# Attention and a mixture of experts on one core: how a pair of heads is turned back, projected and divided

## The chip, the cores and the metric

One core of one Trainium2 chip runs the whole program. The metric is the device time of one execution in microseconds (us); lower is better. TensorE (PE) multiplies and transposes into PSUM, VectorE (DVE) and ScalarE (ACT) read PSUM, GpSimd (POOL) works in SBUF alone, and SyncE (SP) issues most of the transfers.

## What is computed

Attention with rotary embedding over 8 batches, 8 heads, 576 positions and 64 dimensions, and then a top-1 mixture of 8 experts (512 to 1024 to 512) over the 4608 tokens. Cut to what matters:

```
q_rot, k_rot = rotate(q), rotate(k)
scores = q_rot @ k_rot.T / sqrt(64)
attn = exp(scores - max); attn = attn / (sum(attn) + 1e-9)
x = attn @ v                       # to 4608 x 512
logits = x @ w_gate; e = argmax(logits); gate = softmax(logits)[e]
eom = sigmoid(x @ w_output_gate)
out[token] = gate * eom[e] * (relu(x @ w1[e]) @ w2[e])
```

## The kernel before

The program is first attention, then experts. Attention goes through 32 pairs of heads, four to a batch (`NP` = 4). A pair has nine steps; a step computes the scores of 128 queries of one head against all 576 keys (`scores`, L464; one step serves the last 64 queries of both heads, L457), takes their maximum on DVE (`peak`, L470) and the exponential on ACT (`exp`, L479), and one step later DVE transposes the result in blocks of 32 (`turn`, L485). Operands are split into a rounded high part and a remainder, so that each product is three matmuls. Scores have two PSUM buffers; the exponential frees one.

`values` (L507) multiplies the turned exponentials by v. It gives the pair's output with the 2 x 64 dimensions on the partitions and the 576 queries along the free axis, in the one PSUM tile `acc` (4 banks). To store tokens by rows it must be turned back. `evict` (L514 to L516) copies `acc` to SBUF (`ac`) on ACT, as five chunks of queries: four of 128 and one of 64. `back` (L522) turns each chunk and computes its logits in one matmul of 160 moving columns: the chunk is the stationary operand, and the moving operand `ii` is the identity (128 columns) beside the weights of both gates for both heads (32 columns, `BW` = 160 in all). The operands are full fp32, and each such matmul runs as two instructions of TensorE with a load of weights each. `divide` multiplies the result, read from `acc`, by the reciprocal sums `rz` into the token tile `xb`: three instructions on DVE (L530: four chunks, L532: their logits, L535: logits of the fifth chunk) and two on ACT (L539: the fifth chunk, one for each head). Then the `values` of the next pair can use `acc`.

The order of the work is written out by hand. `EVENTS` gives each part a step and a phase. In one step come the scores, the maximum and the exponential, then what is listed in phase 1 (`back` among it), then the `turn` of the step before, then phase 2 (`divide` among it), then phase 3. Within a phase the parts come in the order in which they were listed. Each engine executes its instructions in this order.

Routing (`place`) runs once per batch, spread over the steps of the following pairs with a list of its own (`fs`). Two of its matmuls on TensorE borrow free columns of a later pair's `acc`: the ranks (`s14`, L655 and L656, read on DVE by `s14b`, L660 and L661, which also adds `base`, made on POOL by L643) and the token lists (`s20`, L695, read on DVE by `s21`, L698). Both fall into a step in which a pair is turned back, `s14` and `s20` in phase 1 just ahead of `back`, and their readers in phase 3. With pairs counted from 0, the ranks meet every fourth pair from the sixth (5, 9, ... 29), the lists every fourth from the eighth (7, 11, ... 31). `ones` (L685 on DVE, L687 on POOL) falls into the steps after pairs 6, 10, ... 30. `own` holds the tiles that two pairs use in turn.

Of the kernel before, what the change touches and what calls it, by code (L numbers as in the profile page):

```python
# [10 lines left out]
F32 = mybir.dt.float32  # L11
# [3 lines left out]
AF = mybir.ActivationFunctionType  # L15
ALU = mybir.AluOpType
# [3 lines left out]
S, H, D = 576, 8, 64  # L20
NP = H // 2
DM = H * D
E, FF = 8, 1024
P = 128
HS = S // 2
QM = 512
QR = S - QM
NCH = 5
XW = DM + 1

HL = 2 * E
RW = DM + H * HL

BW = P + 2 * HL
# [8 lines left out]
NB, TAIL, PE_, PO = S // 32, 160, 192, 0  # L43
# [74 lines left out]
def body(ctx, tc, nb, offs, qk, v, rope, cst, gates, w, out):  # L118
    nc = tc.nc
    NT = nb * S  # L120

    def pool(st, n, b, **k):
        return st.enter_context(tc.tile_pool(name=n, bufs=b, **k))


    early, main, scores = ExitStack(), ExitStack(), ExitStack()
    cpool = pool(ctx, "cpool", 1, side="left")
    dpool = pool(ctx, "dpool", 1, space=bass.MemoryType.DRAM)
    px, px2 = pool(ctx, "px", 1, side="left"), pool(ctx, "px2", 2, side="left")
    pa2 = pool(main, "pa", 2, side="left")  # L130
    pp1, pp2 = pool(early, "pp", 1, side="right"), pool(early, "pp2", 2, side="right")
    ps_a = pool(main, "ps_a", 1, space=PSUM, side="left")
    ps_s = pool(scores, "ps_s", 2, space=PSUM, side="right")

    small = Small(ps_s)
    pools = px, px2, pa2, pp1, pp2, ps_s, small, ps_a

    xd = dpool.tile([NT, XW], F32, name="xd")

    nl = E * list_rows(nb) // P  # L140
    lst = [dpool.tile([nl, P], F32, name=f"lst{c}") for c in range(2)]

    first = Pair.first(tc, pools, qk[0, 0], rope)
    ident = cpool.tile([P, P], F32, name="ident")
    make_identity(nc, ident)
    o = offs[C_TRI]
    ct = cpool.tile([P, o], F32, name="ct")
    cc = lambda i: ct[:, offs[i]:offs[i + 1]]

    stage = pa2.tile([P, 2, S], F32, tag="stage", name="stage", bufs=1).rearrange("p a b -> p (a b)")  # L150
    nst = offs[-1] - o
    sc = lambda i: stage[:, offs[i] - o:offs[i + 1] - o]

    ii = cpool.tile([P, NP, BW], F32, name="ii")
    trib = cpool.tile([P, P], BF16, name="trib")
    oneb = cpool.tile([P, P], BF16, name="oneb")
    cnt = cpool.tile([P, E], F32, name="cnt")

    row = cpool.tile([P, nl], BF16, name="row")
    lists = cpool.tile([P, nl], F32, name="lists")  # L160
    zero = stage[:, nst:nst + 256]
    nc.vector.memset(zero, 0.0)
    nc.scalar.dma_start(out=ct, in_=cst[:, 0:o])
    nc.scalar.dma_start(out=stage[:, 0:nst], in_=cst[:, o:])
    nc.scalar.dma_start(out=ii[:, :, P:].rearrange("p n (h x) -> p n h x", h=2), in_=gates)


    consts = [
        lambda: nc.vector.tensor_copy(ii[:, :, 0:P], ident.unsqueeze(1).broadcast_to((P, NP, P))),
        lambda: nc.vector.tensor_copy(trib, sc(C_TRI)),  # L170
        lambda: nc.vector.tensor_copy(oneb, sc(C_ONE)),
        lambda: nc.vector.tensor_copy(row, sc(C_ROW)),
        lambda: (nc.vector.memset(cnt, 0.0), nc.vector.memset(lists, 0.0)),
    ]

    att = Attention(tc, nb, pools, cc, ident, ii, first, trib, oneb, cnt, zero, qk, v, xd, row, lists)
    n0 = slot_counts(nb)[0]
    moe = Moe(tc, nb, (px, px2, small), cc, ident, cnt, w, xd, lists, lst, out)

    if n0:  # L180
        g = att.done(nb - 3) + 1
        for k, f in enumerate(pieces(moe.table0(), 18)):
            att.at(g + k, 2, f)
        att.at(g + 18, 2, moe.fetch)
    att.start(consts)
    for g in range(att.G):
        att.step(g)
    early.close()
    if n0:
        moe.open_right(pool(ctx, "mr", 1, side="right", reuse_waits="tile"))  # L190
        moe.begin0()
    for g in range(att.G, att.G + TURN):
        att.step(g)
    scores.close()
    small.move(pool(ctx, "ps_x", 2, space=PSUM, side="right", reuse_waits="tile"))
    moe.ph = pool(ctx, "ps_h", 1, space=PSUM, side="right", reuse_waits="tile")
    if not n0:
        att.rest(lambda g: True)
        main.close()
        moe.open_right(pool(ctx, "mr", 1, side="right", reuse_waits="tile"))  # L200
        left = []
    else:

        att.rest(lambda g: g <= att.G + 1)
        for u in range(3):
            moe.split(u)
        att.rest(lambda g: g <= att.G + 8)
        for h in range(2):
            moe.turn(0, h)
        for j in range(2):  # L210
            moe.products(0, j)
        att.rest(lambda g: True)
        main.close()
    moe.open_left(pool(ctx, "ml", 1, side="left", reuse_waits="tile"),
                  pool(ctx, "ps_m", 1, space=PSUM, side="left", reuse_waits="tile"))
    if n0:
        left = att.last + pieces(moe.table1(), 60)
    else:
        for f in att.last + pieces(moe.table1(), 60):
            f()  # L220
        moe.fetch()
        moe.begin0()
        moe.begin1()
    moe.run(left)
# [7 lines left out]
class Attention:  # L232


    def __init__(self, tc, nb, pools, cc, ident, ii, first, trib, oneb, cnt, zero, qk, v, xd, row, lists):
        nc = tc.nc
        px, px2, pa2, pp1, pp2, ps_s, small, ps_a = pools
        NT = nb * S
        own = []
        self.inits = []  # L240

        def init(bd, z, rz):
            nc.gpsimd.tensor_copy(bd.rearrange("p a b -> p (a b)"), zero)
            nc.gpsimd.memset(z, 1.0)
            nc.gpsimd.memset(rz, 1.0)

        for i in range(2):
            o = (px.tile([P, 2, P], F32R, name=f"bd{i}"), px.tile([P, 2 * NCH], F32, name=f"z{i}"),
                 px.tile([P, 2 * NCH], F32, name=f"rz{i}"), px.tile([P, 1], F32, name=f"no{i}"))
            self.inits.append(lambda o=o: init(*o[0:3]))  # L250
            own.append(o)
        npair = nb * NP
        self.G, self.pairs = 9 * npair, []
# [88 lines left out]
class Pair:  # L342


    def __init__(self, tc, pools, n, own, ident, ii, rt, qk, v):
        self.tc, self.nc = tc, tc.nc
        self.px, self.px2, self.pa, self.pp1, self.pp2, self.ps_s, _, self.ps_a = pools
        self.bd, self.z, self.rz, self.no = own
        self.n, self.nm, self.hp = n, f"{n}", n % NP
        self.ident, self.ii, self.rt, self.qkd, self.vd = ident, ii, rt, qk, v  # L350
        self.raw = None
# [157 lines left out]
                                 skip_group_check=True)  # L509

    def evict(self):
        ac = self.ac = self.pa.tile([P, NCH, 4, 32], F32, tag="ac", name=f"ac{self.nm}")
        main = self.acc[:, :, 32:TAIL].rearrange("p a (c x) -> p c a x", x=32)
        self.nc.scalar.copy(ac[:, 0:4, :, :], main)  # L514
        self.nc.scalar.copy(ac[0:D, 4, 0:2, :], self.acc[0:D, 0:2, TAIL:PE_])
        self.nc.scalar.copy(ac[D:P, 4, 0:2, :], self.acc[D:P, 2:4, 0:32])  # L516

    def back(self):

        for c in range(NCH):  # L520
            n, o = (P, PO) if c < 4 else (QR, PO + BW)
            self.nc.tensor.matmul(self.acc[0:n, c % 4, o:o + BW], self.ac[:, c, :, :].rearrange("p a x -> p (a x)")[:, 0:n],  # L522
                                  self.ii[:, self.hp, :], start=True, stop=True, skip_group_check=True)

    def divide(self, xb):
        nc, V, acc, rz = self.nc, self.nc.vector, self.acc, self.rz
# [8 lines left out]
        V.tensor_tensor(out=xb[0:QR, 4, l0:l0 + 2 * HL].rearrange("p (h x) -> p h x", x=HL),  # L535
                        in0=last[:, P:BW].rearrange("p (h x) -> p h x", x=HL),
                        in1=rz[0:QR, 8:10].unsqueeze(2).broadcast_to((QR, 2, HL)), op=ALU.mult)
        for h in range(2):
            nc.scalar.activation(xb[0:QR, 4, x0 + h * D:x0 + h * D + D], last[:, h * D:h * D + D], AF.Copy,  # L539
                                 scale=rz[0:QR, 8 + h:9 + h])  # L540


def number(NT, b):
# [5 lines left out]
def place(tc, pools, pairs, b, NT, cc, trib, oneb, cnt, xbs, xd, row, lists):  # L549

    nc = tc.nc
# [70 lines left out]
    def s10():  # L622
        V.tensor_scalar(T["eg"], T["eg"], 1.0, None, op0=ALU.add)

    def s11():
        tt(out=T["eg"], in0=T["eg"], in1=T["sm"], op=ALU.mult)

    def s12():
        nc.vector.reciprocal(T["eg"], T["eg"])
# [36 lines left out]
    def s16():  # L666
        nc.vector.tensor_reduce(new("po", [P, NCH]), T["pr"], axis=AX.X, op=ALU.add)
# [42 lines left out]
    def adds(*cs):  # L710
        return lambda: [add(c) for c in cs]

    fs = [(0, 2, s0), (2, 2, s1), (3, 2, s2), (5, 2, s3), (8, 2, s4), (9, 2, s5), (10, 2, s6), (11, 2, s7), (12, 2, add0),
          (12, 2, adds(1, 2)), (13, 2, adds(3, 4)), (15, 2, s8), (15, 2, base), (17, 1, s14), (17, 3, s14b), (18, 2, s9),
          (19, 2, lambda: (s10(), s11())), (20, 2, s15), (22, 2, lambda: (s16(), s12())), (23, 2, s17), (35, 1, s20), (35, 3, s21)]
    fs += [(26 + c, 3, lambda c=c: ones(c)) for c in range(NCH)]

    if b == NT // S - 2:
# [449 lines left out]
```

## Time and profile before

| | |
|---|---|
| time, median of 3 runs | 1104.14 us (1101.99 to 1106.68) |
| the profiled execution, its own time | 1111.51 us |
| its span, first to last instruction | 1109.7 us |
| PE busy | 1027.9 us (93%) |
| DVE busy | 827.9 us (75%) |
| ACT busy | 644.7 us (58%) |
| POOL busy | 604.1 us (54%) |
| mean granted clock of TensorE | 0.971 |

Busy time is the union of an engine's instructions. Matmuls are pipelined, so that the records of neighbours overlap; what one costs is read from start to start. Loads of weights are listed as PEld. The attention part runs to about 600 us, the experts behind it.

### The profile page before, as it was taken

What the parts mean: (1) busy time and instruction counts of PE and PEld (TensorE: products, weight loads), DVE (VectorE), ACT (ScalarE), POOL (GpSimd) and SP (SyncE); (2) the same over time, 40 slices, a digit from 0 to 9 for tenths busy, and PEclk for the clock granted to TensorE, in tenths of its full rate; (3) what the DMA queues carried; (4) which work ended last, traced back from release to release, by engine and by line L of the source; (5) the groups of instructions that cost most, each with busy time, mean ns of one, the idle gap of its engine ahead of it and who ended that gap; (6) DMA issues with size and microseconds to landing.
All of it is one profiled execution on the core that took longest, in us unless ns stands there. A gap on an engine that the chain in (4) does not pass through costs nothing.

```text
span 1109.7 us, 34896 instructions
## 1 busy us (share of the span) xinstructions
PE 1027.9 (93%) x14465; PEld 890.5 (80%) x14465; DVE 827.9 (75%) x1357; ACT 644.7 (58%) x1345; POOL 604.1 (54%) x592
## 2 busy tenths in 40 slices
PE   3999999999999999999976998899999999999995
PEld 3788877877877787787766987798899889889885
DVE  6788888888888688788764775656767867876782
ACT  3466666666666465566453553455757756766772
POOL 4667887887978688688531051112532632632621
PEclk9999999999999899899888998999999999999998
DMA  5545555555746455545266585556887888888870
GB/s 184 162 129 164 167 165 145 152 166 159 199 126 174 114 167 173 130 145 159 51 184 210 199 302 184 190 171 193 301 291 252 286 286 292 265 305 304 256 274 27
DMA packets 58562, 216.48 MB, mean 195 GB/s; under 512 B 9405, under 2 KB 10012, under 8 KB 54304
## 3 DMA queue, kind: packets, MB, share of 16 engines
q1 hardware_dynamic: 50304, 194.03, 55.9%
q0 software_dynamic: 6496, 18.92, 4.8%
q8 instruction: 115, 1.88, 0.7%
q10 hardware_dynamic: 1600, 1.26, 0.4%
q14 instruction: 47, 0.39, 0.1%
HBM read 196.04 MB, written 20.24 MB: 195 GB/s over the span
## 4 chain that ended last, share of the span: by engine, by line
PE 65%; DVE 12%; issue 10%; DMA 6%; ACT 4%; POOL 2%; SPq 1%; POOLq 0%; ACTq 0%; DVEq 0%
PE py L1045 15%; PE sc L464 15%; PE acc L507 14%; PE ph L1002 11%; PE ph L994 4%; DVE m L470 3%; DVE pt L485 3%; DMA out<-y,0idx 3%; ACT pm L479 2%; PE acc L522 2%; PE sc L457 2%; PE mtp L980 1%; DVE wl L966 1%; DMA v<-in_v 1%; DVE xb L530 1%
## 5 line engine op out<-in xcount | busy, mean ns | idle before, releaser
L479 ACT ACTIVATE pm<-sc,m 128x576 f32<-128x576 f32 x288 | 213.5, 741 | 192.9 <-DVE m L470 191.3
L966 DVE TENSOR_TENSOR wl<-wr,wh 128x1024 fp32r<-128x1024 f32 x183 | 254.6, 1403 | 48.1 <-ACT wh L964 46.5
L470 DVE TENSOR_REDUCE m<-sc 128x1 f32<-128x576 f32 x288 | 213.2, 740 | 85.8 <-PE sc L464 70.7
L464 PE MATMUL sc<-kh,q 64*128 64x288 f32 x1024 | 227.7, 330 | 26.4 <-ACT pm L479 11.7
L507 PE MATMUL acc<-pt,v 32*64 32x160 f32 (+1 forms) x9216 | 203.0, 303 | 19.2 <-DMA v<-in_v 5.2
L485 DVE STREAM_TRANSPOSE pt<-pm 128x576 f32<-128x576 f32 x288 | 220.0, 764 | 0.3 <-ACT pm L479 0.3
L1045 PE MATMUL py<-wh,ht 128*128 128x512 f32 x640 | 214.9, 400 | 0.0
L964 ACT CAST wh<-wr 128x1024 fp32r<-128x1024 f32 x208 | 212.7, 1050 | 0.4 <-DMA wr<-in_w 0.4
L464 PEld LDWEIGHTS sc<-kh,q 64*128 64x128 f32 x1024 | 154.1, 195 | 69.5 <-ACT pm L479 26.1
L507 PEld LDWEIGHTS acc<-pt,v 32*64 32x64 f32 x9216 | 163.2, 135 | 43.8 <-issue 21.3
L1002 PE MATMUL ph<-xt,wh 128*128 128x256 f32 x896 | 166.4, 289 | 7.3 <-DVE ht L1020 5.8
L413 POOL TENSOR_TENSOR raw<-raw,rt 128x1152 f32<-128x1152 f32 x62 | 164.1, 2647 | 8.3 <-DMA raw<-in_qk 8.0
L1002 PEld LDWEIGHTS ph<-xt,wh 128*128 128x128 f32 x896 | 143.7, 197 | 9.7 <-issue 6.1
L1045 PEld LDWEIGHTS py<-wh,ht 128*128 128x128 f32 x640 | 120.6, 188 | 24.8
L1002 PE MATMUL ph<-xt,wl 128*128 128x256 f32 x448 | 128.5, 287 | 0.0
L1045 PE MATMUL py<-wl,ht 128*128 128x512 f32 x320 | 125.7, 393 | 0.0
L966 POOL TENSOR_TENSOR wl<-wr,wh 128x1024 fp32r<-128x1024 f32 x25 | 61.3, 2450 | 110.6 <-ACT wh L964 108.2
L464 PE MATMUL sc<-kl,q 64*128 64x288 f32 x512 | 112.6, 302 | 0.6 <-issue 0.6
L417 POOL TENSOR_TENSOR raw<-raw 128x576 f32<-128x576 f32 x62 | 88.1, 1421 | 2.4
L1019 ACT ACTIVATE ht<-ph 128x512 fp32r<-128x512 f32 x56 | 33.5, 598 | 96.1 <-PE ph L1002 96.1
L1002 PEld LDWEIGHTS ph<-xt,wl 128*128 128x128 f32 x448 | 88.6, 198 | 0.0
L464 PEld LDWEIGHTS sc<-kl,q 64*128 64x128 f32 x512 | 86.0, 196 | 0.9 <-issue 0.9
(245 smaller groups left out, 1329.3 us busy)
## 6 DMA issues: line engine op xcount, KB each, us to landing
wr<-in_w SPq DMA_DIRECT2D x208, 512.0 KB, 5.5
raw<-in_qk SPq DMA_DIRECT2D x64, 576.0 KB, 4.7
v<-in_v SPq DMA_DIRECT2D x128, 288.0 KB, 5.2
xd<-xb SPq DMA_DIRECT2D x16, 513.0 KB, 4.9
xd<-xb SPq DMA_DIRECT2D x8, 128.2 KB, 4.3
rt<-in_rope ACTq DMA_DIRECT2D x1, 576.0 KB, 5.6
xg<-xd,2idx POOLq DMA_INDIRECT x18, 6.8
out<-y,2idx POOLq DMA_INDIRECT x18, 5.2
```

Of the source, the lines that this page charges most:

```text
L413: self.eng(eng).tensor_tensor(out=rv, in0=rv, in1=self.rt[:, 2 * t:2 * t + 2, x], op=ALU.mult)
L417: self.eng(eng).tensor_tensor(out=r[:, 2 * t, x], in0=r[:, 2 * t, x], in1=r[:, 2 * t + 1, x], op=ALU.add)
L464: nc.tensor.matmul(ps[:, a, :HS], self.q[r, w, c * P:c * P + P], mov[r, a * HS:a * HS + HS], start=(n == 0), stop=(n == 2))
L470: nc.vector.tensor_reduce(self.m[i], ps[:, :, :HS], axis=AX.XY, op=ALU.max, negate=True)
L479: nc.scalar.activation(pe.rearrange("p (a b) -> p a b", a=2), self.ps[i][:, :, :HS], AF.Exp, bias=self.m[i], scale=1.0, accum_out=self.z[: ...
L485: self.nc.vector.transpose(out=self.pt[:, st[0] + 5 * st[1] if st else 4, :], in_=self.pc.pop(i))
L507: nc.tensor.matmul(self.acc[h * D:h * D + D, a, o:o + 32 * n], self.v[r, h, j, :], self.pt[r, u:u + n, 32 * j:32 * j + 32], start=(j == 0) ...
L964: self.nc.scalar.copy(wh, r)
L966: eng.tensor_tensor(out=wl, in0=r, in1=wh.bitcast(F32), op=ALU.subtract)
L994: nc.tensor.matmul(ph[:, 0, :], st[:, dc, 0:P], mv[:, dc, :], start=(n == 0), stop=(n == 11))
L1002: nc.tensor.matmul(ph[:, f, :], st[:, dc, fs], mv[:, dc, :], start=(n == 0), stop=(n == 11))
L1045: self.nc.tensor.matmul(py[h], st[:, f, hs], mv, start=(f == 0 and n == 0), stop=(f == 7 and n == 2))
```

## The change

`back` becomes two loops: five transposing instructions of TensorE (the chunk against the 128-column identity `ident`), and then five matmuls that multiply the same chunks by the gate weights alone, with 32 moving columns. `ii` holds only those 32 columns for each of the four pairs of a batch, and the DVE copy of the identity into it (L169) is gone. The fifth chunk is handled with 128 columns like the others: `ac` becomes a tile of `own`, whose fifth chunk POOL fills with zeros once at the start. The two divisions on ACT become one on DVE. `s14b` and `s21` move from phase 3 to phase 2, where they are listed ahead of `divide`.

```diff
-    ii = cpool.tile([P, NP, BW], F32, name="ii")
+    ii = cpool.tile([P, NP, 2 * HL], F32, name="ii")
...
-    nc.scalar.dma_start(out=ii[:, :, P:].rearrange("p n (h x) -> p n h x", h=2), in_=gates)
+    nc.scalar.dma_start(out=ii.rearrange("p n (h x) -> p n h x", h=2), in_=gates)
...
-        lambda: nc.vector.tensor_copy(ii[:, :, 0:P], ident.unsqueeze(1).broadcast_to((P, NP, P))),
...
+        def init(bd, z, rz, ac):
+            nc.gpsimd.memset(ac[:, NCH - 1, :, :], 0.0)
...
-                 px.tile([P, 2 * NCH], F32, name=f"rz{i}"), px.tile([P, 1], F32, name=f"no{i}"))
+                 px.tile([P, 2 * NCH], F32, name=f"rz{i}"), px.tile([P, NCH, 4, 32], F32, name=f"ac{i}"))
...
-        ac = self.ac = self.pa.tile([P, NCH, 4, 32], F32, tag="ac", name=f"ac{self.nm}")
+        ac = self.ac
...
+        parts = []
         for c in range(NCH):
-            n, o = (P, PO) if c < 4 else (QR, PO + BW)
-            self.nc.tensor.matmul(self.acc[0:n, c % 4, o:o + BW], self.ac[:, c, :, :].rearrange("p a x -> p (a x)")[:, 0:n],
-                                  self.ii[:, self.hp, :], start=True, stop=True, skip_group_check=True)
+            o = PO if c < 4 else PO + BW
+            parts.append((self.acc[:, c % 4, o:o + BW], self.ac[:, c, :, :].rearrange("p a x -> p (a x)")))
+        for out, x in parts:
+            self.nc.tensor.transpose(out=out[:, 0:P], in_=x, identity=self.ident)
+        for out, x in parts:
+            self.nc.tensor.matmul(out[:, P:], x, self.ii[:, self.hp, :], start=True, stop=True, skip_group_check=True)
...
-        for h in range(2):
-            nc.scalar.activation(xb[0:QR, 4, x0 + h * D:x0 + h * D + D], last[:, h * D:h * D + D], AF.Copy,
-                                 scale=rz[0:QR, 8 + h:9 + h])
+        V.tensor_tensor(out=xb[0:QR, 4, x0:x0 + P].rearrange("p (h x) -> p h x", x=D),
+                        in0=last[:, 0:P].rearrange("p (h x) -> p h x", x=D),
+                        in1=rz[0:QR, 8:10].unsqueeze(2).broadcast_to((QR, 2, D)), op=ALU.mult)
...
-(17, 1, s14), (17, 3, s14b), ... (35, 1, s20), (35, 3, s21)]
+(17, 1, s14), (17, 2, s14b), ... (35, 1, s20), (35, 2, s21)]
```

## Rows read from the trace of the kernel before

**Rows 1.** Windows: start:end, us, busy PE, PEld, DVE, ACT, POOL, clock, DMA, GB/s

```profile
54.00:600.00 546.00, 512.12 (x10973) 427.00 (x10970) 436.26 (x829) 322.44 (x868) 400.98 (x455) 0.97 0.55 154
372.00:392.00 20.00, 20.00 (x354) 16.73 (x353) 12.47 (x23) 9.92 (x27) 10.29 (x12) 0.75 0.32 93
```

**Rows 2.** Waits: engine and line <- releaser: us in total, times, longest

```profile
ACT xb L539 <- DVE xb L535: 39.3, 26, 10.4
...
PEld acc L507 <- ACT xb L539: 10.4, 18, 2.0
```

**Rows 3.** Timeline of pair 8's turning back: start, us, ..., [idle before]

```profile
185.83 0.30 PEld L522 LDWEIGHTS acc<-ii,ac 128*128 128x128 f32 x2 [0.17 <-issue]
...
185.83 1.77 PE L522 MATMUL acc<-ii,ac 128*128 128x160 f32 x10
...
187.53 0.29 PEld L464 LDWEIGHTS sc<-kh,q 64*128 64x128 f32 x2 [0.23 <-issue]
```

**Rows 4.** Lines L522 and L980: ns min/median/max, first and last start

```profile
L522 PEld LDWEIGHTS acc<-ii,ac x320: 132/190/337, 54.7 to 599.6; 128*128 128x128 f32 x128, 128*64 128x64 f32 x32
...
L980 PE MATMUL mtp<-ident,xg x160: 270/272/330, 588.6 to 1077.5; 128*128 128x128 f32 x160
```

**Rows 5.** Timeline: eight transposing instructions of the experts' part

```profile
588.61 1.09 PE L980 MATMUL mtp<-ident,xg 128*128 128x128 f32 x8
```

**Rows 6.** Timeline: a 40-column matmul of routing ahead of pair 5's turning back

```profile
134.86 0.18 PE L656 MATMUL acc<-ohb,trib 128*128 128x40 bf16 x1
...
134.87 0.30 PEld L522 LDWEIGHTS acc<-ii,ac 128*128 128x128 f32 x2
```

**Rows 7.** Timeline of pair 0's division and of what follows

```profile
56.96 0.65 DVE L530 TENSOR_TENSOR xb<-acc,rz 128x512 f32<-128x512 f32 x1
...
57.54 0.28 DVE L532 TENSOR_TENSOR xb<-acc,rz 128x128 f32<-128x128 f32 x1
...
57.74 0.17 DVE L535 TENSOR_TENSOR xb<-acc,rz 64x32 f32<-64x32 f32 x1
57.84 0.73 DVE L470 TENSOR_REDUCE m<-sc 128x1 f32<-128x576 f32 x1
...
58.00 0.51 ACT L539 ACTIVATE xb<-acc,rz 64x64 f32<-64x64 f32 x2 [0.71 <-DVE xb L535]
...
58.56 0.51 PEld L507 LDWEIGHTS acc<-pt,v 32*64 32x64 f32 x32 [0.40 <-ACT xb L539]
59.03 0.74 ACT L479 ACTIVATE pm<-sc,m 128x576 f32<-128x576 f32 x1
```

**Rows 8.** Timeline of pair 5, which the ranks meet

```profile
136.94 0.19 POOL L643 TENSOR_TENSOR base<-cnt,ct 128x8 f32<-128x8 f32 x1
...
138.72 0.20 DVE L660 TENSOR_TENSOR pr<-acc,base 128x40 f32<-128x40 f32 x1 [0.70 <-ACT xb L539]
...
138.90 0.74 DVE L470 TENSOR_REDUCE m<-sc 128x1 f32<-128x576 f32 x1
139.21 0.40 PEld L507 LDWEIGHTS acc<-pt,v 32*64 32x64 f32 x24 [0.96 <-ACT bd L441]
```

**Rows 9.** Timeline of pair 7, which the lists meet

```profile
171.53 0.69 DVE L530 TENSOR_TENSOR xb<-acc,rz 128x512 f32<-128x512 f32 x1 [0.53 <-PE acc L522]
...
173.14 0.46 DVE L698 TENSOR_TENSOR lists<-acc,lists 128x288 f32<-128x288 f32 x1 [0.64 <-ACT xb L539]
173.51 0.75 DVE L470 TENSOR_REDUCE m<-sc 128x1 f32<-128x576 f32 x1
173.67 0.46 PEld L507 LDWEIGHTS acc<-pt,v 32*64 32x64 f32 x28 [1.04 <-PE sc L464]
```

**Rows 10.** Timeline of DVE in pair 6: its two idle stretches from 151 us

```profile
150.93 0.76 DVE L470 TENSOR_REDUCE m<-sc 128x1 f32<-128x576 f32 x1 [0.84 <-PE sc L464]
...
165.95 0.76 DVE L470 TENSOR_REDUCE m<-sc 128x1 f32<-128x576 f32 x1 [1.15 <-PE sc L464]
```

**Rows 11.** Waits from 366 to 373 us, ahead of the slow stretch

```profile
PE sc L464 <- issue: 1.4, 1, 1.4
```

More of the change, by code (lines that the diff above doesn't have):

```diff
@@ L240, in __init__ @@
         self.inits = []
-        def init(bd, z, rz):
+        def init(bd, z, rz, ac):
+            nc.gpsimd.memset(ac[:, NCH - 1, :, :], 0.0)
             nc.gpsimd.tensor_copy(bd.rearrange("p a b -> p (a b)"), zero)
@@ L248, in __init__ @@
             o = (px.tile([P, 2, P], F32R, name=f"bd{i}"), px.tile([P, 2 * NCH], F32, name=f"z{i}"),
-                 px.tile([P, 2 * NCH], F32, name=f"rz{i}"), px.tile([P, 1], F32, name=f"no{i}"))
-            self.inits.append(lambda o=o: init(*o[0:3]))
+                 px.tile([P, 2 * NCH], F32, name=f"rz{i}"), px.tile([P, NCH, 4, 32], F32, name=f"ac{i}"))
+            self.inits.append(lambda o=o: init(*o))
             own.append(o)
@@ L347, in __init__ @@
         self.px, self.px2, self.pa, self.pp1, self.pp2, self.ps_s, _, self.ps_a = pools
-        self.bd, self.z, self.rz, self.no = own
+        self.bd, self.z, self.rz, self.ac = own
         self.n, self.nm, self.hp = n, f"{n}", n % NP
@@ L713, in place @@
     fs = [(0, 2, s0), (2, 2, s1), (3, 2, s2), (5, 2, s3), (8, 2, s4), (9, 2, s5), (10, 2, s6), (11, 2, s7), (12, 2, add0),
-          (12, 2, adds(1, 2)), (13, 2, adds(3, 4)), (15, 2, s8), (15, 2, base), (17, 1, s14), (17, 3, s14b), (18, 2, s9),
-          (19, 2, lambda: (s10(), s11())), (20, 2, s15), (22, 2, lambda: (s16(), s12())), (23, 2, s17), (35, 1, s20), (35, 3, s21)]
+          (12, 2, adds(1, 2)), (13, 2, adds(3, 4)), (15, 2, s8), (15, 2, base), (17, 1, s14), (17, 2, s14b), (18, 2, s9),
+          (19, 2, lambda: (s10(), s11())), (20, 2, s15), (22, 2, lambda: (s16(), s12())), (23, 2, s17), (35, 1, s20), (35, 2, s21)]
     fs += [(26 + c, 3, lambda c=c: ones(c)) for c in range(NCH)]
```

## The prediction

> **What bounds the kernel now.** I read the page first, then windows, the chain of waits and the waits by line, then the timeline of single pairs. The page gives PE 93% of the span. In attention, from 54 to 600 us, PE is busy 512 of 546 us, DVE 436, POOL 401 and ACT 322 [rows 1]. PE carries attention, then, and whatever stops it is paid. One stop recurs in every pair: the `values` of the next pair wait until `acc` is free, and its last reader is the division of the fifth chunk on ACT. The waits name it 18 times for 10.4 us, and that division itself waits 39.3 us for the division on DVE ahead of it [rows 2].
>
> The reader should see how one pair runs. In pair 0 [rows 7] DVE starts the division at 56.96 and begins the next maximum at 57.84; ACT starts its two copies at 58.00, is done at 58.51, and PE begins to load for `values` at 58.56, after 0.40 us idle. A change of tile shape costs PE 0.17 to 0.23 us idle anyway [rows 3]; 0.23 us is the stop. Where the ranks are read behind the division (pairs 5, 9, ... 29), DVE too stands still, 0.70 us, until ACT is done, and PE is idle 0.96 us [rows 8], 0.79 more than the shape change. Where the lists are read (7, 11, ...), DVE stands 0.64 and PE 1.04 us [rows 9], an excess of 0.87. Taken together the excess is 10.4 - 18 x 0.17 = 7.3, 7 x 0.79 = 5.5 and 7 x 0.87 = 6.1 us: 18.9 us that could at most be gained at this place.
>
> **Turning back on PE.** Before: from the first load to the load of the next scores 187.53 - 185.83 = 1.70 us [rows 3] for ten instructions of 160 columns. After: five transposing instructions and ten of 32 columns. Eight transposing instructions of the same form take 1.09 us to the end of the last, which is 0.272 long [rows 4, 5]: (1.09 - 0.272) / 7 = 0.117 us from start to start, 0.58 for five. For 32 moving columns with a load of 128 full fp32 columns the trace has no row. From below: one column streams in 0.117 / 128 = 0.9 ns, 32 in 0.03 us, if the loads were hidden. From above: load plus stream. A load takes 0.11 us: the second of two starts 0.30 - 0.19 = 0.11 after the first [rows 3, 4]. The nearest row is the 40-column matmul ahead of pair 5's turning back: behind it the first load of L522 lasts until 134.87 + 0.30 - 0.19 = 134.98, 0.12 us after that short matmul began [rows 6]. So a short matmul does not cover the next load, though it runs while it is fetched; I take the load, 0.11 us, for each of the ten, with 0.03 and 0.14 as bounds: 1.1 us (0.3 to 1.4). The fifth chunk, now 128 wide, needs no change of shape of its own; the last one, to the scores, is 0.1 to 0.2 us from a short matmul. Sum 0.58 + 1.1 + 0.1 = 1.78, against 1.70. The 0.08 is no more than these rows resolve (the 0.117 contains a first load, which the 1.70 has too), and in the plain pairs part of it would be absorbed by the stop at `acc`; I book no change. The bounds are 0.7 less to 0.5 more a pair.
>
> One instruction's length is 0.272 us [rows 4] and its neighbours start 0.117 us apart [rows 5]; I priced it by the spacing. The Trainium skill, "TensorE: Matmul & The Clock Gate", Part 4 (PE-mode transpose), gives about 275 ns for one of 128 x 128 within a kernel: the trace agrees on the length, not on what one costs in a row of them. At 275 ns each, the page's estimate would be 1.38 us for the five instead of 0.58.
>
> **The division.** ACT loses 0.51 us a pair, DVE gains one instruction of 128 elements on 64 partitions. Nearest is L532, also 128 elements to a partition: 0.28 long, 0.20 from its start to the next [rows 7]. Bounds: 0.10, the step of L535, and 0.28. I take 0.20 for DVE's queue and 0.28 for its end. Now class by class, since what is freed at `acc` comes back only as far as the next exponentials follow: the next maximum is queued behind the new instruction, its exponential behind that maximum, and two score buffers later PE waits for that exponential.
>
> - *Plain pairs and those with two small reductions ahead of the division (0 to 3, 4, 8, ... 28: 11).* The new division ends at 57.84 + 0.28 = 58.12, before PE wants `acc` (58.56 - 0.23 = 58.33): 0.23 us free. The next maximum ends 0.20 later, at 57.84 + 0.73 + 0.20 = 58.77; its exponential, which ACT's copies and the casts behind them held until 59.03, can start about 58.85, 0.18 earlier. Worth 0.17 each: 1.9 us.
> - *Ranks (7 pairs).* `s14b` now stands ahead of the division on DVE and needs POOL's `base`, which ends at 136.94 + 0.19 = 137.13 [rows 8], when the division would start. So it delays: 137.20, 0.20 for L660 and L661, 0.88 for L530 to L535 (56.96 to 57.84 in [rows 7]), 0.20: the next maximum at 138.48, against 138.90. PE may start at about 138.6 against 139.21. The smaller counts: 0.42 x 7 = 2.9 us.
> - *Lists (6 pairs; the seventh, 31, lies behind the last scores).* DVE is idle 0.53 us ahead of the division, until the turning back is done [rows 9]. L530 started only at the end of the fifth chunk's matmul, of which it reads nothing; I take it that a reader of `acc` waits for all of `back`, so L698 too starts at 171.53, not in the idle time. It holds DVE 173.51 - 173.14 = 0.37 us; then 0.88 and 0.20: the next maximum at 172.98, against 173.51. 0.5 x 6 = 3.0 us. If it can use the idle time, 0.9 x 6.
> - *`ones` (6, 10, ... 30: 7).* DVE has no idle time between 150.93 and 165.95 but the one that ends there [rows 10]; the new 0.20 us is pushed through to PE: 0.2 x 7 = 1.4 us lost.
>
> **What hides the rest.** The zero fill and the shorter transfer of gate weights fall into the start, where POOL does nothing until the first rotation; without that cover they cost under 1 us once. L169 goes once. `ac` still alternates between two tiles, so `evict` waits for nothing new.
>
> **Sum.** -1.9 - 2.9 - 3.0 + 1.4 = -6.4 us. The profiled execution's 1111.5 becomes 1105.1; the median lies 7.4 us below it, so 1104.1 becomes 1097.7, 0.6% faster.
>
> **The rivals.**
> *All of the stop is gained*: DVE's idle time and ACT's relief let the exponentials keep up with PE, and nothing comes back later. For it speaks that DVE is idle ahead of the lists; against it the ordering of maximum and exponential in [rows 7]. Up to 18.9 us: 1085 to 1094. Chance 0.2.
> *The gain is eaten*: PE's ten short instructions cost load plus stream (0.5 a pair, of which the plain pairs feel some 0.2), or DVE, with 32 x 0.20 = 6.4 us more, becomes the engine that PE waits for, so that one stop replaces another. For it speaks DVE's unbroken work in [rows 10]; against it that DVE loses 0.70 and 0.64 us of idle time in 13 pairs. Between 3 us gained and 5 lost: 1101 to 1109. Chance 0.2.
> *TensorE's clock falls (slower)*: attention is granted 0.97 of full speed on the mean, but the stretch from 372 to 392 us only 0.75, half of it at 1.2 GHz [rows 1], after PE had been idle 1.4 us [rows 11]. Such a stretch loses about 20 x 0.25 = 5 us. If transposing and 32-column instructions leave the array as good as idle for 1.7 us in each pair, more such falls follow; three more outweigh the gain (3 x 5 - 6.4 = 9 us slower), 1110 to 1125. Against it: dense scores stand on both sides, and PE's longest regular stops get shorter. Chance 0.06. The Trainium skill says in the same Part 4 that a transpose does not count as busy time for the clock; no run here shows it yet.
> *Transposing instructions don't overlap here (slower)*: if each of the five costs its length, 0.272, instead of 0.117, `back` takes 5 x 0.155 = 0.78 us more, 25 us over 32 pairs: about 1122. Against it [rows 5], where eight of them run overlapped. Chance 0.02. This is what the page's 275 ns (the Trainium skill, Part 4 as above) would amount to.
>
> **How the numbers follow.** The forecast, a gain of 3 to 10 us, has 0.52. Half a per cent, 5.5 us, is about what a measurement of this kernel can tell from no change. Of the forecast's chance 0.35 lies above that and 0.17 below. Faster 0.35 + 0.2 = 0.55; the same 0.17 + 0.2 = 0.37; slower 0.08. The range takes in most of the first rival and of the second: 1087 to 1105.5. The forecast's own range is 1094 to 1101.
>
> **What would show each step.** Turning back again about 1.7 us from first load to the next scores, with short instructions 0.11 us apart: if 0.03 or 0.14, the load's price was wrong. L539 gone; no wait of L660 and L698 for ACT; `values` in plain pairs with the bare 0.17 to 0.23 us of idle time; in pairs 7, 11, ... L698 starting at the end of `back`. DVE's work some 6 us more, ACT's some 16 less. The prediction is wrong if scores after `values` wait longer for exponentials than now, if POOL's `base` comes later than the turn, or if the granted clock of attention leaves 0.97.

## The result, and the profile after

The changed kernel takes 1091.89 us, the median of 20 runs (1082.45 to 1107.2); the kernel before takes 1105.27 us, run beside it (20 runs, 1099.77 to 1112.85). The ratio is 0.9864 (95% interval 0.9843 to 0.9886): 1.4% faster, 13 to 15 us. That lies inside the range of 1087 to 1105.5 and on the side that had the larger chance, but the gain is about twice the 6.4 us forecast, and the time lies below the forecast's own range of 1094 to 1101. The profiled execution took 1088.35 us, its span is 1086.5 us, and the mean granted clock is 0.977, against 0.971 before.

The page's line of busy times, changed kernel:

```profile
PE 1018.3 (94%) x14625; PEld 898.2 (83%) x14625; DVE 828.6 (76%) x1388; ACT 627.9 (58%) x1281; POOL 606.5 (56%) x594
```

ACT has lost the 16 us that were expected. DVE has 0.7 us more, not 6, though it executes 31 more instructions (32 divisions, less the copy at the start); over pairs 0 to 26 it has 386.01 - 382.60 = 3.4 us more (windows below), and the rest of the program takes most of that back.

The timeline of pair 0, changed kernel, answers to [rows 3, 7]. The code lies four lines lower: L522 has become L525 (transposing) and L527 (32 columns), L530 to L535 are L534 to L539, and the new division is L542. Columns: start, us, engine, line, idle time before.

```profile
54.66 0.53 PEld L525 LDWEIGHTS acc<-ident,ac 128*128 128x128 f32 x5 [0.16 <-issue]
54.67 0.77 PE L525 MATMUL acc<-ident,ac 128*128 128x128 f32 x5
55.16 1.20 PEld L527 LDWEIGHTS acc<-ii,ac 128*128 128x128 f32 x10
55.27 1.20 PE L527 MATMUL acc<-ii,ac 128*128 128x32 f32 x10
56.40 0.30 PEld L464 LDWEIGHTS sc<-kh,q 64*128 64x128 f32 x2
...
57.79 0.27 DVE L542 TENSOR_TENSOR xb<-acc,rz 64x128 f32<-64x128 f32 x1
57.99 0.73 DVE L470 TENSOR_REDUCE m<-sc 128x1 f32<-128x576 f32 x1
58.28 1.35 PEld L507 LDWEIGHTS acc<-pt,v 32*64 32x64 f32 x80 [0.16 <-issue]
58.81 0.74 ACT L479 ACTIVATE pm<-sc,m 128x576 f32<-128x576 f32 x1 [1.08 <-DVE m L470]
```

Turning back takes 56.40 - 54.66 = 1.74 us, as before (1.70). The ten loads of the short matmuls take 1.20 us; less the 0.19 that a single load lasts and by nine steps, that is 0.112 us from start to start. On DVE the new division takes 57.99 - 57.79 = 0.20 us of the queue. `values` now starts after 0.16 us, the bare change of tile shape; the stop at `acc` has gone. The next exponential starts 58.81 - 54.67 = 4.14 us after turning back begins, before 59.03 - 54.71 = 4.32: 0.18 earlier.

A ranks pair (5) and a lists pair (7), changed kernel, the same view; they answer to [rows 8, 9]:

```profile
135.52 0.19 POOL L647 TENSOR_TENSOR base<-cnt,ct 128x8 f32<-128x8 f32 x1
135.75 0.20 DVE L664 TENSOR_TENSOR pr<-acc,base 128x40 f32<-128x40 f32 x1
135.94 0.68 DVE L534 TENSOR_TENSOR xb<-acc,rz 128x512 f32<-128x512 f32 x1
137.17 1.35 PEld L507 LDWEIGHTS acc<-pt,v 32*64 32x64 f32 x80 [0.29 <-PE sc L464]
...
170.16 0.46 DVE L702 TENSOR_TENSOR lists<-acc,lists 128x288 f32<-128x288 f32 x1 [1.35 <-PE acc L527]
170.54 0.68 DVE L534 TENSOR_TENSOR xb<-acc,rz 128x512 f32<-128x512 f32 x1
171.77 1.35 PEld L507 LDWEIGHTS acc<-pt,v 32*64 32x64 f32 x80 [0.52 <-PE sc L464]
```

PE's idle time ahead of `values` falls from 0.96 to 0.29 us and from 1.04 to 0.52. The reader of the ranks follows POOL's `base` at once, and the reader of the lists starts only when the last instruction of `back` is done, though the lists were in `acc` earlier.

What a pair costs is read from one turning back to the next, in pairs with a granted clock of 1.00. Windows of the kernel before, in order: pair 1 (plain), 4 (two small reductions ahead of the division), 5 (ranks), 14 (`ones`), 15 (lists), and the stretch of pairs 0 to 26. Columns as in [rows 1].

```profile
70.69:86.67 15.98, 15.80 (x353) 13.28 (x352) 13.45 (x23) 10.48 (x28) 11.08 (x8) 1.00 0.53 149
118.64:134.89 16.25, 15.86 (x356) 13.31 (x355) 13.82 (x26) 10.48 (x28) 13.36 (x21) 1.00 0.53 148
134.89:151.37 16.48, 15.57 (x356) 13.11 (x355) 13.74 (x27) 10.57 (x29) 12.50 (x17) 1.00 0.52 148
285.56:303.32 17.76, 17.05 (x359) 14.01 (x358) 16.37 (x35) 11.19 (x29) 17.38 (x15) 1.00 0.77 216
303.32:319.43 16.11, 15.02 (x354) 12.62 (x353) 12.98 (x23) 10.02 (x29) 12.34 (x14) 1.00 0.51 136
54.71:516.25 461.54, 440.05 (x9547) 366.63 (x9546) 382.60 (x710) 285.82 (x769) 367.35 (x401) 0.98 0.56 157
```

The same of the changed kernel, and one row more, its pair 13:

```profile
70.41:86.15 15.74, 15.62 (x359) 13.56 (x358) 13.57 (x24) 9.98 (x26) 11.09 (x8) 1.00 0.55 150
117.63:133.49 15.86, 15.60 (x360) 13.49 (x360) 13.88 (x27) 9.99 (x26) 13.34 (x21) 1.00 0.53 150
133.49:149.33 15.84, 15.42 (x360) 13.33 (x360) 13.89 (x28) 10.05 (x27) 12.48 (x17) 1.00 0.53 150
282.88:300.82 17.94, 17.13 (x363) 14.38 (x362) 16.55 (x36) 10.65 (x27) 17.33 (x15) 1.00 0.75 218
300.82:316.41 15.59, 15.02 (x358) 12.98 (x358) 13.09 (x24) 9.51 (x27) 12.33 (x14) 1.00 0.48 135
54.67:498.17 443.50, 429.98 (x9683) 369.53 (x9682) 386.01 (x737) 271.78 (x715) 366.68 (x401) 0.99 0.58 163
265.47:282.88 17.41, 17.32 (x360) 15.02 (x359) 13.94 (x28) 10.05 (x27) 12.44 (x17) 0.90 0.50 138
```

Class by class a pair is shorter by 0.24, 0.39, 0.64, -0.18 and 0.52 us. Over 4, 7, 7, 7 and 6 pairs that is 1.0 + 2.7 + 4.5 - 1.3 + 3.1 = 10.0 us. Pair 28 does not follow its class, though no fall of the clock lies in it: it lasts 16.85 us before and 17.15 after, which takes 0.7 us off the sum. The other 4 to 6 us go with the granted clock. Its median over the runs is 0.975, against 0.970 before, and over 46 timed executions of the kernel before an execution is 0.9 us shorter for each 0.001 of mean granted clock. That is a correlation; it does not say what moves the clock.

The last row is a pair of the ranks class that lost 17.41 - 15.84 = 1.57 us to that clock: 0.90 on its mean, with no stop of PE to speak of (busy 17.32 of 17.41 us). Such pairs become the main point below.

The waits of the changed kernel answer to [rows 2]; columns as there:

```profile
PEld sc L464 <- ACT pm L479: 33.0, 67, 2.0
...
DVE lists L702 <- PE acc L527: 14.2, 7, 10.1
```

The two waits for ACT's division are gone. Scores wait for the exponential 33.0 us instead of 26.1: a part of the freed time is given back there. The lists wait for turning back for 14.2 us in all, but 10.1 of that is one wait, in pair 31, behind the last scores; the other six come to 4.1.

### The profile page after: what moved, and what is told of

Same layout as the page of the kernel before. It is cut to its first block, busy times and chain, and to the rows that moved or that the text cites. A ratio compares the mean times of both kernels' runs of the same rounds, so it can differ in the third digit from the quotient of the medians.

```text
span 1086.5 us, 35130 instructions
## 1 busy us (share of the span) xinstructions
PE 1018.3 (94%) x14625; PEld 898.2 (83%) x14625; DVE 828.6 (76%) x1388; ACT 627.9 (58%) x1281; POOL 606.5 (56%) x594
## 4 chain that ended last, share of the span: by engine, by line
PE 66%; DVE 13%; ACT 6%; issue 6%; POOL 5%; DMA 3%; ACTq 0%; POOLq 0%; SPq 0%; DVEq 0%
PE py L1049 18%; PE ph L1006 15%; PE sc L464 12%; PE acc L507 11%; PE ph L998 4%; DVE m L470 4%; ACT pm L479 4%; DVE pt L485 3%; POOL raw L413 2%; PE mtp L984 2%; DVE xb L534 1%; DVE wl L970 1%; ACT kh L387 1%; DMA xd<-xb 1%; DMA v<-in_v 1%
## 5 line engine op out<-in xcount | busy, mean ns | idle before, releaser
L970 DVE TENSOR_TENSOR wl<-wr,wh 128x1024 fp32r<-128x1024 f32 x183 | 251.1, 1384 | 47.4 <-ACT wh L968 46.6
L464 PE MATMUL sc<-kh,q 64*128 64x288 f32 x1024 | 222.1, 327 | 30.1 <-ACT pm L479 15.7
L507 PE MATMUL acc<-pt,v 32*64 32x160 f32 (+1 forms) x9216 | 200.2, 303 | 4.4 <-issue 1.9
L464 PEld LDWEIGHTS sc<-kh,q 64*128 64x128 f32 x1024 | 148.7, 192 | 66.7 <-ACT pm L479 33.0
L1006 PE MATMUL ph<-xt,wh 128*128 128x256 f32 x896 | 170.1, 292 | 5.6 <-DVE ht L1024 4.6
L1006 PEld LDWEIGHTS ph<-xt,wh 128*128 128x128 f32 x896 | 146.4, 200 | 9.0 <-issue 4.7
L1024 DVE SCALAR_TENSOR_TENSOR ht<-ph,ht 128x512 fp32r<-128x512 f32 x56 | 38.7, 691 | 63.5 <-ACT ht L1023 63.3
```

The costliest lines, as they stand in the source:

```text
L464: nc.tensor.matmul(ps[:, a, :HS], self.q[r, w, c * P:c * P + P], mov[r, a * HS:a * HS + HS], start=(n == 0), stop=(n == 2))
L507: nc.tensor.matmul(self.acc[h * D:h * D + D, a, o:o + 32 * n], self.v[r, h, j, :], self.pt[r, u:u + n, 32 * j:32 * j + 32], start=(j == 0) ...
L970: eng.tensor_tensor(out=wl, in0=r, in1=wh.bitcast(F32), op=ALU.subtract)
L1006: nc.tensor.matmul(ph[:, f, :], st[:, dc, fs], mv[:, dc, :], start=(n == 0), stop=(n == 11))
```

## The experiments

**The theory and its rivals at the start.** The theory: the whole gain is ACT's division leaving the path, and the new turning back changes nothing. Rivals: the new turning back, or the earlier reading of ranks and lists, brings a good part of it; or TensorE's clock does. Ratios are to the kernel before, run beside each on the same chip.

**Division and readers, without the new turning back.** The kernel before with these edits:

```diff
-        for h in range(2):
-            nc.scalar.activation(xb[0:QR, 4, ...], last[:, h * D:h * D + D], AF.Copy, scale=rz[0:QR, 8 + h:9 + h])
+        V.tensor_tensor(out=xb[0:QR, 4, ...], in0=last[:, 0:P]..., in1=rz[0:QR, 8:10]..., op=ALU.mult)
...
-(17, 3, s14b), ... (35, 3, s21)
+(17, 2, s14b), ... (35, 2, s21)
```

> The kernel before with the division of the fifth chunk on DVE and the two readers of routing ahead of the division; turning back stays as it was (ten instructions of 160 columns). Theory A (the gain is the wait for acc, and the new turning back is neutral): the whole gain of the change is here already, 12 to 16 us less than before, ratio 0.986 to 0.989. Theory B (the gain is in the new turning back): within 3 us of before, ratio 0.997 to 1.000.

Measured: 1092.85 us, ratio 0.9842 (0.9806 to 0.9877). The whole gain is there without the new turning back.

**The new turning back alone.** The changed kernel with both divisions on ACT again and the readers back in phase 3.

```diff
-        V.tensor_tensor(out=xb[0:QR, 4, ...], in0=last[:, 0:P]..., in1=rz[0:QR, 8:10]..., op=ALU.mult)
+        for h in range(2):
+            nc.scalar.activation(xb[0:QR, 4, ...], last[:, h * D:h * D + D], AF.Copy, scale=rz[0:QR, 8 + h:9 + h])
...
-(17, 2, s14b), ... (35, 2, s21)
+(17, 3, s14b), ... (35, 3, s21)
```

> The kernel before with the new turning back alone (five transposing instructions, ten of 32 columns, fifth chunk widened); division on ACT and readers last, as before. Theory A: turning back costs 1.735 us a pair in place of 1.70, so 0 to 2 us more than before, ratio 0.999 to 1.002. Theory B: 12 to 16 us less than before. Theory C (the excess over the sum comes from TensorE's clock, which short and transposing instructions would lift or lower): a granted clock that differs from that of before by more than 0.003, and a time that follows it.

Measured: 1119.94 us, ratio 1.0077 (1.004 to 1.0115): slower, which of the three expectations only the third, the clock, allows. Undisturbed pairs last what they lasted before (15.99, 16.25, 16.47, 16.12 us by class). But in five pairs before 500 us (1, 10, 14, 17, 22) the clock falls for some 3.4 us; pair 1 is 1.6 us longer by it. Its windows in this experiment, cut at the start of the next pair's `values` (74.30) and about where the clock is back:

```profile
70.64:74.30 3.66, 3.66 (x28) 3.33 (x27) 3.66 (x8) 2.04 (x6) 2.61 (x3) 1.00 0.91 229
74.30:78.00 3.70, 3.52 (x84) 3.08 (x84) 2.40 (x5) 2.74 (x8) 1.40 (x1) 0.55 0.33 67
78.00:88.22 10.22, 10.22 (x250) 8.63 (x249) 7.42 (x11) 5.68 (x15) 7.07 (x4) 1.00 0.41 133
```

The first row is the turning back and the scores behind it; PE is busy without a gap. Then, 0.4 us after the next pair's `values` begin, the granted clock goes to half, 1.2 GHz, for some 3.4 us, and comes back to 2.4 GHz. Over all its runs the median clock is 0.964, against 0.971 of the kernel before beside it; by the slope above that is some 6 of the 9 us lost. So the third theory, in this form, went on to the next experiments: the new turning back makes TensorE's clock fall.

**The changed kernel with the readers last.**

```diff
-(17, 2, s14b), ... (35, 2, s21)
+(17, 3, s14b), ... (35, 3, s21)
```

> The changed kernel with the two readers of routing behind the division again (phase 3). Theory A1 (they stood still only because ACT divided; once DVE divides, their place matters little): within 2 us of the changed kernel, ratio to before 0.986 to 0.989, and DVE idles under 0.1 us ahead of them. Theory A2 (their move ahead of the division is a part of the gain): 13 pairs lose 0.4 to 0.8 us again, 5 to 10 us more than the changed kernel, ratio 0.991 to 0.996.

Measured: 1097.31 us, ratio 0.9872 (0.9831 to 0.9913), the same as the changed kernel. Lists pairs last 15.59 us as there, ranks pairs 15.73 instead of 15.84: reading the ranks early costs 0.1 us a pair, the wait for `base`. The move of the readers is worth nothing once the division is off ACT.

**The changed kernel with ACT dividing.**

```diff
-        V.tensor_tensor(out=xb[0:QR, 4, ...], in0=last[:, 0:P]..., in1=rz[0:QR, 8:10]..., op=ALU.mult)
+        for h in range(2):
+            nc.scalar.activation(xb[0:QR, 4, ...], last[:, h * D:h * D + D], AF.Copy, scale=rz[0:QR, 8 + h:9 + h])
```

> The changed kernel with the fifth chunk divided on ACT again, readers ahead of the division as changed. If the division on DVE is what frees acc: plain pairs wait 0.23 us for acc again, and 10 to 14 us of the gain are gone, ratio 0.996 to 1.000. If the move of the readers alone gives half: ranks and lists keep 0.3 to 0.5 us a pair each, ratio 0.992 to 0.995.

Measured: 1122.46 us, ratio 1.0125 (1.0089 to 1.0162), slower than any value that was expected. It has nine of the short falls by 503 us. Windows of this experiment: an undisturbed pair (8), three with a fall (1, 9 and 17), and the stretch of pairs 0 to 26:

```profile
190.16:206.39 16.23, 15.86 (x361) 13.71 (x360) 13.80 (x26) 10.47 (x28) 13.34 (x21) 1.00 0.53 148
...
70.23:87.80 17.57, 17.41 (x359) 15.02 (x358) 13.47 (x23) 10.48 (x28) 11.09 (x8) 0.90 0.47 136
206.39:224.18 17.79, 17.33 (x361) 15.01 (x360) 13.86 (x27) 10.57 (x29) 12.46 (x17) 0.90 0.48 135
342.74:360.54 17.80, 17.32 (x360) 14.99 (x359) 13.87 (x27) 10.57 (x29) 12.56 (x18) 0.90 0.47 134
54.26:515.92 461.66, 445.33 (x9683) 382.37 (x9682) 383.74 (x710) 285.74 (x769) 367.69 (x402) 0.97 0.57 156
```

**The readers alone.** The kernel before with

```diff
-(17, 3, s14b), ... (35, 3, s21)
+(17, 2, s14b), ... (35, 2, s21)
```

It differs from the experiment above in the turning back alone.

> The kernel before with one edit: the readers of routing ahead of the division (phase 2). It differs from the fourth run (ACT divides, readers moved, new turning back) in the form of turning back alone. If the new turning back costs time through TensorE's clock: 1 to 4 us less than before here, ratio 0.996 to 0.999, with at most two stretches at half clock before 500 us, against nine there. If ACT's division behind the moved readers was the cause of that run's loss: ratio 1.008 or more here too.

Measured: 1110.35 us, ratio 0.9962 (0.9935 to 0.999). Windows of the same three pairs and of the stretch:

```profile
70.69:86.67 15.98, 15.80 (x353) 13.25 (x352) 13.47 (x23) 10.46 (x28) 11.08 (x8) 1.00 0.52 148
201.56:217.78 16.22, 15.63 (x356) 13.14 (x355) 13.86 (x27) 10.56 (x29) 12.49 (x17) 1.00 0.52 150
334.62:350.84 16.22, 15.63 (x355) 13.15 (x354) 13.86 (x27) 10.56 (x29) 12.55 (x17) 1.00 0.51 147
54.70:513.49 458.79, 439.54 (x9548) 365.78 (x9547) 383.24 (x710) 285.59 (x769) 368.83 (x403) 0.98 0.56 158
```

None of its falls before 500 us lies behind a turning back; two of 6.8 us (368 and 440 us) follow stops of PE. Work on the other engines is the same to 0.1 us in each of these pairs. The old form is not free of such falls, though. In the profile of the kernel before, pair 21 lasts 18.10 us instead of 16.48: the clock falls 4.6 us after its turning back starts, as `values` begin, here behind a stop of 0.7 us of PE. Windows of that pair and of the fall:

```profile
408.29:426.39 18.10, 17.36 (x355) 14.64 (x354) 13.77 (x27) 10.57 (x29) 12.54 (x17) 0.91 0.48 131
412.75:416.50 3.75, 3.75 (x85) 3.31 (x86) 2.43 (x5) 2.22 (x6) 1.77 (x4) 0.54 0.09 21
```

So the short falls come far more often with the new form of `back`, and with ACT dividing it makes the kernel 1.6% slower (1.0125 against 0.9962), about 18 us. The median clock of the runs is 0.959 there and 0.9695 here, which by the slope above is 9 to 10 of them. The rest does not show as clock and was not settled.

**The division alone.** The kernel before with only the division on DVE (the first half of the first diff).

> The kernel before with one edit: the fifth chunk divided on DVE. Turning back and the readers' place stay. If the wait for ACT was the whole matter: 14 to 18 us less than before, ratio 0.983 to 0.988, like the kernel with the readers moved too, and pairs that the ranks meet are some 0.1 us shorter than there, since POOL's base is not waited for. If the readers' move is needed as well: ratio 0.990 or more.

Measured: 1092.32 us, ratio 0.9816 (0.9783 to 0.9849), the lowest of all ratios, with that of the next experiment. The stretch of pairs 0 to 26 has a granted clock of 1.00:

```profile
55.05:497.06 442.01, 429.25 (x9547) 358.16 (x9546) 385.32 (x737) 271.81 (x715) 366.65 (x401) 1.00 0.58 164
```

Pairs last 15.74 (plain), 15.73 (ranks) and 15.56 us (lists), as in the changed kernel or a little less. One edit of the four gives everything.

**The fifth chunk widened, in the old form.** The experiment above with `ac` from tiles that POOL fills with zeros, and

```diff
-            n, o = (P, PO) if c < 4 else (QR, PO + BW)
-            self.nc.tensor.matmul(self.acc[0:n, c % 4, o:o + BW], self.ac[:, c, :, :]...[:, 0:n], self.ii[:, self.hp, :], ...)
+            o = PO if c < 4 else PO + BW
+            self.nc.tensor.matmul(self.acc[:, c % 4, o:o + BW], self.ac[:, c, :, :]..., self.ii[:, self.hp, :], ...)
```

> The kernel before with the fifth chunk divided on DVE and widened by zeros, but turned back in ten instructions of 160 columns as before; readers last. The change of tile shape ahead of the fifth chunk goes: 1.56 us in place of 1.70 for turning back. If turning back counts in full on PE: 4 us less than with the division alone, ratio 0.980 to 0.984. If DVE and ACT set the pace behind the division: no change against the division alone, 0.984 to 0.988. No stretch at half clock before the seventh batch.

Measured: 1093.05 us, ratio 0.9816 (0.9784 to 0.9848), no gain over the division alone. Lists pairs are 15.43 instead of 15.56 us; the other classes do not change. Turning back takes 1.55 us there instead of 1.70, and nearly nothing of it reaches the end.

**Which of the two loops makes the clock fall.** Two kernels, both with ACT dividing. The first keeps the transposing instructions and widens the short matmuls, so that each chunk is turned twice; for that `ii` holds the identity again, and `ac` lies in another pool:

```diff
-            self.nc.tensor.matmul(out[:, P:], x, self.ii[:, self.hp, :], ...)
+            self.nc.tensor.matmul(out, x, self.ii[:, self.hp, :], ...)
```

> The fourth run (ACT divides, readers moved, transposing instructions) with the ten instructions behind the transposing ones widened from 32 to 160 columns, so that they turn the chunk once more: more work on PE, 0.25 us a pair. If the clock falls because the 32-column instructions leave the array idle while weights load: the falls before 500 us are gone (two at most, against nine), and in spite of the work the time is lower, ratio 0.998 to 1.006. If it falls because of the transposing instructions: falls stay, ratio 1.012 to 1.020. If the clock has nothing to do with it: 0.25 x 32 = 8 us more than there, ratio 1.015 to 1.022.

Measured: 1119.31 us, ratio 1.0045 (1.0018 to 1.0072). Turning back takes 2.06 us, 0.3 more than with short matmuls, yet the ratio is lower than 1.0125, and the profile has no fall before 519 us. Pairs 1 and 9 and the stretch, windows of this experiment:

```profile
70.88:86.85 15.97, 15.80 (x358) 13.58 (x357) 13.45 (x23) 10.46 (x28) 11.08 (x8) 1.00 0.54 150
203.26:219.49 16.23, 15.66 (x361) 13.46 (x360) 13.88 (x27) 10.55 (x29) 12.51 (x17) 1.00 0.53 149
54.89:506.71 451.82, 433.76 (x9683) 369.92 (x9682) 383.57 (x710) 285.41 (x770) 367.68 (x402) 1.00 0.57 161
```

Against the readers alone the ratio is 0.8% higher, at the same median clock (0.970). Its lists pairs, 0.35 us longer, explain 2 of these 9 us; the rest is open. So not all that the new form costs shows as clock.

The second keeps the short matmuls and turns by ordinary matmuls with the identity:

```diff
-            self.nc.tensor.transpose(out=out[:, 0:P], in_=x, identity=self.ident)
+            self.nc.tensor.matmul(out[:, 0:P], x, self.ident, start=True, stop=True, ...)
```

> The fourth run (ACT divides, readers moved) with the five transposing instructions replaced by matmuls with the identity (ten instructions of 128 columns, 0.11 us each), the ten of 32 columns kept: 0.55 us more work on PE a pair. If the 32-column instructions alone let the clock fall: several falls of 3.4 us before 500 us stay (four or more), ratio 1.012 or more. If it takes the transposing ones as well: at most two such falls, and only the longer work remains, some 0.3 us a pair beyond what the wait for acc absorbs, ratio 1.003 to 1.010.

Measured: 1134.91 us, ratio 1.02 (1.0162 to 1.0238). The profiled execution was the fastest of its runs, 1122.13 us, and has no fall behind a turning back; two falls (at 166 us for 3.4 us and at 309 us for 10.2 us) follow stops of PE. So in the profiles the short falls come with transposing instructions and 32-column matmuls together, and none with one of the two alone. For the short matmuls this is weak evidence: it is one execution, the fastest, and four of its other five show clocks of 0.959 to 0.966, hardly above the 0.953 to 0.964 with ACT dividing. That the transposing instructions are needed is therefore not shown. The price, too, is more than the 0.05 to 0.6 us by which its undisturbed pairs are longer. Why is open.

**Both again, side by side.** The changed kernel unaltered and the division alone, on another chip.

> The changed kernel, unaltered, beside the next one on one chip: ratio 0.984 to 0.989 as before, with one to three short falls of the clock before 500 us.

> The kernel before with the fifth chunk divided on DVE alone, beside the changed kernel on one chip. If the old form of turning back is better because it keeps the clock: 2 to 6 us less than the changed kernel, ratio 0.980 to 0.985, and no short falls behind a turning back before 500 us. If the two are equal: within 2 us.

Measured: 1103.0 us, ratio 0.9878 (0.9838 to 0.9917), median clock 0.9675; and 1095.51 us, ratio 0.9826 (0.9797 to 0.9854), median clock 0.974. The changed kernel's profile shows two short falls in attention behind a turning back (at 204 and 320 us), the other's shows none. The division alone is ahead by 0.5%, as it is by the ratios of the first runs, taken on different chips (0.9816 and 0.9864); here the intervals overlap, so that this difference is likely, not certain.

Over all profiles, falls that begin 3.8 to 4.6 us after a turning back starts, in pairs 0 to 26: one in 162 pairs of the six kernels with the old form (one of them with the fifth chunk widened), nineteen in 135 pairs of the five profiles with transposing instructions and 32-column matmuls (two, two, five, one and nine). Widening alone is thus not what brings them.

## Why the prediction was right or wrong

**Turning back: booked at no change; right in its length.** 1.74 us for 1.70. The short matmuls' loads are 0.112 us apart, the price taken from [rows 3, 4, 6], not 0.03 or 0.14; the five transposing instructions take 0.77 us to the end of the last, (0.77 - 0.272) / 4 = 0.12 apart. The instruction is 0.27 us long, as the Trainium skill, "TensorE: Matmul & The Clock Gate", Part 4 (PE-mode transpose), says (about 275 ns), and the spacing shows that this length is not what one costs in a row. The rival by that rule is out.

**The wait for ACT's division and the new instruction: right.** The waits of [rows 2] are gone, the new step is 0.20 us of DVE's queue and 0.27 long (booked 0.20 and 0.28), and the next exponential starts 0.18 us earlier, as worked out. Lists pairs gained 0.52 (booked 0.5), `ones` pairs lost 0.18 (booked 0.2). The reader of the lists does wait for all of `back`, and the ranks' reader for `base`.

**The terms that were mis-sized.** Plain pairs 0.24 instead of 0.17, pairs 4, 8, ... 28 0.39 instead of 0.17, ranks pairs 0.64 instead of 0.42. The step that failed is "what is freed at `acc` comes back only as far as the next exponentials follow". That holds at that place, to 0.01 us in pair 0, but the pair has other stops behind it, and part of the earlier start is kept there too. I see this in the periods; which later stop gives how much in each class was not measured alone. In sum 9 to 10 us instead of 6.4.

**The readers' move: wrongly thought to matter.** The prediction worked the ranks and the lists through the new order. With the division on DVE the order is worth nothing, or 0.1 us a ranks pair on the wrong side; with ACT dividing it is worth 0.4% (0.9962).

**The first rival** (all of the stop gained, 1085 to 1094) has the time right, 1091.9, but not by its mechanism: the exponentials do not keep up, scores wait 33.0 us for them, against 26.1 before. That was one of the prediction's signs of being wrong; it came, and the time fell all the same. The stated range holds the measured time only because it was stretched for this rival, and that is luck. **The gain is eaten**: it is not: DVE has 3.4 us more work over pairs 0 to 26, but no class but `ones` got longer.

**TensorE's clock falls**: given 0.06, and this mechanism is there. The new turning back alone makes the kernel 0.8% slower, and 1.6% between the two kernels that differ in it alone. Part of these losses does not show as clock. The size was wrong: a fall behind `back` costs 1.6 us, not 5, and there are five to nine of them where the old wait stays. In the changed kernel the profile has two, and its other profile, of another chip, has two as well. What else removes them there was not settled: the division on DVE shortens the stop ahead of `values`, at which the falls begin, but no run changed that stop by itself. A stop is not needed: ahead of the fall in the changed kernel's pair 20 the last matmul of the scores ends at 384.92 + 0.42 = 385.34 us, and `values` start at 385.34. Timeline of PE, and the window in which the clock goes down:

```profile
384.92 0.42 PE L464 MATMUL sc<-kh,q 64*128 64x288 f32 x2
385.34 2.88 PE L507 MATMUL acc<-pt,v 32*64 32x160 f32 x80
385.50:385.75 0.25, 0.25 (x20) 0.25 (x22) 0.25 (x1) 0.00 (x0) 0.25 (x1) 0.57 2.21 442
```

The Trainium skill says in the same Part 4 that a transpose does not count as PE-busy in the same way. If that alone made the clock fall, the five would be enough; in the profile they are not, since with 160-column matmuls behind the same five no fall follows before 519 us.

**The missing term** is thus that the parts are not independent: the change consists of one edit that gives 1.8% and another that, likely, takes about 0.5% of it back. The clock is most of that as far as the last two runs show: 0.9675 against 0.974 is by the slope 6 of the 7.5 us between them. The forecast hit the side, with a gain of 6.4 where the edit that pays is worth some 20 us by its ratios (1 - 0.9816 of 1113.69). About ten of these are the pairs, counted by class as above; the remainder goes with the clock and with short interruptions of PE that differ from execution to execution, and these I could not take apart.

## What to carry to other kernels

When a small operation on a second engine is the last reader of a buffer that the bounding engine waits for, move that operation first and measure it alone: here it is the whole gain. Read the granted clock pair by pair before trusting a sum of busy times, for an exchange that leaves TensorE's time unchanged (1.74 for 1.70 us) can still cost 0.8%, most of it through its clock. And when a change has several edits, price them as a group too: a gain in one can hide the loss of another.

## What was not expected of the hardware

The granted clock fell to 1.2 GHz without any long stop of TensorE ahead of it: 3.66 us of unbroken work, a short stop at the start of `values`, then some 3.4 us at 0.5. All falls of this kind in the changed kernel, in the new turning back alone and in the kernel with ACT dividing begin there, 3.8 to 4.6 us after a turning back by transposing instructions and 32-column matmuls starts, in two to nine pairs of 27; the other pairs of the stretch, with the same instructions, show no such fall. With the old form there is one in 162 pairs. A matmul with 32 moving columns behind a full fp32 load of 128 columns follows its neighbour after 0.112 us, no less than two such loads did before (0.11). And the reader of the lists, which lie in their own columns of `acc`, starts only behind the last matmul of a turning back that it does not use: 4.1 us of waiting in six pairs, and 10.1 in the last. Whether the chip or the program's own semaphores ask for that, the trace does not say.
